# Tile 3's attention result turned by a DMA instead of TensorE, its low part one slot behind the join

## The chip, the core and the metric

The kernel runs on one core of a Trainium2 chip. The metric is the device time of one execution in microseconds (us), median over runs. TensorE (PE in the profile, its weight loads PEld) multiplies matrices, VectorE (DVE), ScalarE (ACT) and GpSimd (POOL) work on elements, SyncE (SP) issues nearly all DMAs. Each engine runs its own instructions in program order and waits on semaphores for the others.

## What is computed

A transformer block on 2048 positions of 512 numbers: attention with 32 heads of 16 numbers over 8 positions, two apart, then an MLP with a squared relu of 1792 hidden numbers. The reference, cut:

```python
def _A_ref(x, wqkv, wo):                    # H = 32, Dh = 16, W = 8, dil = 2
    q, k, v = split(x @ wqkv)
    idx = pos[:, None] - (arange(W) * dil)[None, :]      # 8 earlier positions
    logits = einsum("bhsd,bhswd->bhsw", q, k[idx]) * Dh ** -0.5
    attn = softmax(where(idx >= 0, logits, -1e9))
    o = einsum("bhsw,bhswd->bhsd", attn, v[idx])
    return o.reshape(B, S, D) @ wo
def _B_ref(x, w1, b1, w2, b2):
    r = relu(x @ w1 + b1)
    return (r * r) @ w2 + b2
h = x + _A_ref(layernorm(x), wqkv, wo)
out = h + _B_ref(layernorm(h), w1, b1, w2, b2)
```

## The kernel before

The 2048 positions are 16 tiles of 128. Every float32 product is made of three: each operand is split into a high part in a form that TensorE takes at full rate (a cast, `hi`, L151, on ScalarE) and a low part, the rest (a subtraction, `lo`, L154, on VectorE or GpSimd), and `mm3` (L221) multiplies high by high, low by high and high by low, 12 matmuls of 512 columns for a tile.

The work has two stages. In the first, TensorE makes q, k and v of all tiles, four tiles ahead and then two at a time (`first_phase`, L1040, for tiles 4 and 5 up to 14 and 15). In the second, the MLP runs over four sub-blocks of four tiles. Attention itself is elementwise work: VectorE multiplies and reduces (`dots`, `weigh`), GpSimd adds up (`add_up`), and it runs through the first stage and most of the second as a stream of steps beside the matmuls. Windows of k and v are read back from HBM for it by SP.

A tile's way from attention to the MLP: its result o is transposed, split into oh and ol, multiplied by wo (`wo_product`, L703), added to the residual (h), normalized (hn), transposed again and split into the parts hh and hl that the MLP's first product moves (in the tiles named big_l there). The product's order is set by `lows_last`: for tile 3, whose number is not in `OV`, first oh by wo's high part, then ol by wo's high part, then oh by wo's low part.

There are two ways to transpose o:

- By TensorE (`o_T`, L605): four transposes of 128x128 through the identity into PSUM, then the cast and the subtraction read PSUM.
- By DMA: `o_split` (L642) lets ScalarE write the 16-bit halves of the float32 numbers into two planes (tile pl), `turn_dma` (L631) transposes the planes back into o by a transposing DMA from SP, `o_join` (L647) lets ScalarE put the halves together again in pl, after which the cast and the subtraction read SBUF.

Before, tiles 0 to 3 go by TensorE and tiles 4 to 15 by DMA.

The order of the instructions is set by slots, stretches of TensorE work. In the first stage a slot is half of a 12-matmul product. What is to be done beside is put in lists: `at` runs at the slot's end, before the attention steps, `midway` (list `amid`) amid these steps, and `after` behind them. `end_slot` (L122) then lets `pump` (L420) append attention steps until VectorE's planned time catches up with TensorE's planned time:

```python
    def end_slot(pe):
        now["pe"] += pe
        run(due)
        pump()
        run(amid)
        run(late)
        now["slot"] += 1
```

`transposes` (L201) books 0.44 us of planned TensorE time, so the number of transposes also decides how many attention steps a slot takes. In `first_phase`, k counts the slots from the start of tiles 12 and 13: `OT` gives the slots in which tiles 0 to 3 are turned (4, 5, 10, 12) and `WO` those of their wo products (7, 9, 13, 15).

Of the kernel before, what the change touches and what calls it, by code (L numbers as in the profile page):

```python
# [19 lines left out]
R = 4  # L20
# [20 lines left out]
WO = 7, 9, 13, 15  # L41
HT = 20, 20, 21, 23
HK = (12, 18), (14, 19)
W2 = (18,)
LH = 3, 4, 10, 11
OP = 6, 7, 12, 13
# [12 lines left out]
def block_kernel(ctx, tc, x, wqkv, wo, w1, b1, w2, b2, out):  # L59
# [42 lines left out]
    def row(name, shape=(P, D), dt=F32):  # L102
        return work.tile(list(shape), dt, name=name, tag="row", bufs=ROWS)
# [9 lines left out]
    def at(delta, fn, *a):  # L113
        due.setdefault(now["slot"] + delta, []).append((fn, a))

    def after(delta, fn, *a):
        late.setdefault(now["slot"] + delta, []).append((fn, a))
# [4 lines left out]
# [7 lines that stand above are left out]
# [7 lines left out]
    def dve(t):  # L136
        now["dve"] += t
# [63 lines left out]
    def transposes(src, banks="tr"):  # L201
        tr = turn[banks].tile("tr").rearrange("p (k c) -> p k c", k=KB)
        for k in range(KB):
            nc.tensor.transpose(tr[:, k, :], src[:, k * P:(k + 1) * P], ident)  # L204
        now["pe"] += 0.44
        return tr
# [5 lines left out]
    def hi_T(tr, h_dst):  # L212
        for d, src in parts(tr, h_dst):
            hi(d, src)
# [205 lines left out]
    def pump(until=None):  # L420

        while (done[until] < G) if until is not None else (now["dve"] < now["pe"]):
            if until is None and now["dve"] > now["pe"] - HALF:
                run(amid)
            todo = sums[:]
            sums.clear()
            t = next(stream, "end")
            for a in todo:
                add_up(*a)
            if t == "end":  # L430
                now["dve"] = 1e9
                return
            if t is None:
                now["dve"] = max(now["dve"], now["pe"])
                return
            dve(t * SLOW[min(now['sub'] + 1, 2)])
# [40 lines left out]
    def x_T(t):  # L477
        tr = transposes(xt.pop(t))
        xT[t] = row("xh", (P, KB, P), F32R), row("xl", (P, KB, P), F32R)
        at(0, hi_T, tr, [xT[t][0]])  # L480
        (midway if t >= 6 else after)(0, lo_T, tr, [xT[t][0]], [xT[t][1]])
# [61 lines left out]
    def qkv_of(t, c, mid):  # L543

        ps = turn["mm"].tile("mm")
        xh, xl = xT[t]
        cs = slice(c * D, (c + 1) * D)
        mm3(ps, lambda k: xh[:, k, :], lambda k: xl[:, k, :],
            lambda k: wq_h[:, k, cs], lambda k: wq_l[:, k, cs], mid, 3 * KB // 2,
            lows_last=True)  # L550
        at(1, evac, t, 0, c, ps)
# [43 lines left out]
    oT = {}  # L595
# [9 lines left out]
    def o_T(t):  # L605
        s, j = divmod(t, RI)
        pump(until=s)
        tr = transposes(o_t[s][:, j, :])
        if t % R == RI:

            ohl = att.tile([P, 2, KB, P], F32R, name="ohl", tag="o", bufs=3)
            oT[t] = ohl[:, 0], ohl[:, 1]
        else:
            oT[t] = row("oh", (P, KB, P), F32R), row("ol", (P, KB, P), F32R)
        at(0, hi_T, tr, [oT[t][0]])
        at(0, lo_T, tr, [oT[t][0]], [oT[t][1]])
# [19 lines left out]
    def turn_join(key):  # L636
        src, pl = planes[key]
        nc.scalar.copy(halves_of(pl).rearrange("p two n -> p n two"),
                       two_planes(src).rearrange("p two n -> p n two"))
        planes[key] = pl.rearrange("p (k c) -> p k c", k=KB)  # L640
# [6 lines left out]
    def o_join(t, n=0):  # L647
        turn_join(("o", t))
        tr = planes.pop(("o", t))
        if t % R == RI:  # L650
            ohl = att.tile([P, 2, KB, P], F32R, name="ohl", tag="o", bufs=3)
            oT[t] = ohl[:, 0], ohl[:, 1]
        else:
            oT[t] = row("oh", (P, KB, P), F32R), row("ol", (P, KB, P), F32R)
        hi_T(tr, [oT[t][0]])
        (at if n or t >= 12 else midway)(n, lo_T, tr, [oT[t][0]], [oT[t][1]])

    def h_split(t):
        turn_split(("h", t), hn.pop(t))
# [43 lines left out]
    def wo_product(t, slots):  # L703
        ps = turn["mm"].tile("wo")
        oh, ol = oT.pop(t)
        mm3(ps, lambda k: oh[:, k, :], lambda k: ol[:, k, :],
            lambda k: wo_h[:, k, :], lambda k: wo_l[:, k, :], lows_last=t in OV)
        for n, (fn, a) in zip(slots, ((h_add, (t, ps)), (h_norm, (t,)), (add_b2, (t,)),
                                      (spill, (t,)))):
            (at if fn is h_add or fn is h_norm and t >= 14  # L710
             else midway if fn is h_norm and t in (6, 10) else after)(n + (fn is add_b2), fn, *a)
# [6 lines left out]
    def h_T(t):  # L718
        if t // R == R - 1:
            return last_h_T(t)  # L720
        tr = transposes(hn.pop(t), "mm")
        i = t % R
        hs_, ls_ = [a[:, :, i] for a in hh], [a[:, :, i] for a in hl]
        if len(turn["mm"].tags) > 2:
            at(0, hi_T, tr, hs_)
        else:
            due.setdefault(now["slot"], []).insert(0, (hi_T, (tr, hs_)))
        at(0, lo_T, tr, hs_, ls_)
# [281 lines left out]
    for n in range(16):  # L1010
        gp, t = divmod(n, 4)
# [28 lines left out]
    def first_phase(t0):  # L1040
        def chores(m):
            if t0 + 3 < 16:
                if m in (0, 2):
                    at(0, x_stats, t0 + 2 + m // 2)

                early = t0 == 12
                if m + early in ((4, 6) if t0 == R else (6, 7)):
                    at(0, x_norm, t0 + 2 + (m + early) // 7 if t0 > R else t0 + m // 2)
                if m in XT[early]:
                    x_T(t0 + 2 + XT[early].index(m))  # L1050
            if t0 + 5 < 16 and m in (6, 9):
                at(0, load_x, t0 + 2 + m // 3)
            if jobs and m % 3 == 0:
                at(0, weight_job)
            k = t0 // 2 * 12 - 72 + m
            if k == 19:
                dve(HOLD)
            for t in range(R):
                if k == OT[t]:
                    at(0, load_h, t)  # L1060
                    o_T(t)
                if t in HV and k == HK[t][0]:
                    at(0, h_split, t)
                    after(0, turn_dma, ("h", t))
                if t in HV and k == HK[t][1]:
                    at(0, turn_join, ("h", t))
                if k == WO[t]:
                    wo_product(t, (1, 3, 4, 6))
                    now["pe"] += 2.73
                if k == HT[t]:  # L1070
                    (at(0, h_parts, t) if t in HV else h_T(t))
            if k in W2:
                at(0, load_w2, W2.index(k))

        def half(m):
            end_slot(1.37)
            chores(m)

        for n in range(6):
            chores(2 * n)  # L1080
            qkv_of(t0 + n % 2, n // 2, lambda: half(2 * n + 1))
            end_slot(1.37)
# [40 lines left out]
    for u in range(R - 1):  # L1123
# [11 lines left out]
        for i in js:  # L1135
            t = R * (u + 1) + i
# [158 lines left out]
```

## Time and profile before

| | us |
|---|---|
| median of 3 runs | 501.18 |
| lowest and highest of them | 501.14, 502.29 |
| the profiled execution | 500.91 |
| its span, first to last instruction | 499.1 |
| TensorE busy in the span | 494.2 |
| VectorE busy | 383.7 |
| GpSimd busy | 354.6 |
| ScalarE busy | 305.7 |

The granted TensorE clock was 1.00 of full speed over the whole span. Busy time is summed over the span; which engine sets the time in a stretch is read from the chain and from the waits. All times below are from the span's start.

### The profile page before, as it was taken

Reading aid. Unit: us, or ns where it says so; the run is one execution under the profiler, and the core shown is the slowest. Engines: PE = TensorE matmul, PEld = TensorE weight load, DVE = VectorE, ACT = ScalarE, POOL = GpSimd, SP = SyncE. Lnnn points to the kernel's source line nnn. Section 1 sums busy time; section 2 is a strip of 40 time slices with the busy share of each in tenths; the row PEclk is TensorE's granted clock in tenths of the full one; section 3 lists DMA queues with packets and bytes.
Section 4 is the critical chain, followed back from the end, with each engine's and each line's share of the span. In section 5 each row is a group of like instructions: output and inputs, shape, how many; then the busy total and the mean of one; then the engine's idle time right before and its main releaser. Section 6 shows DMA issues by size and latency. Waiting matters only on the chain.

```text
span 499.1 us, 7514 instructions
## 1 busy us (share of the span) xinstructions
PE 494.2 (99%) x2411; PEld 420.6 (84%) x2411; DVE 383.7 (77%) x526; ACT 305.7 (61%) x543; POOL 354.6 (71%) x429
## 2 busy tenths in 40 slices
PE   8999999999999999999999999999999999999997
PEld 7998888888888888888888888888888888998986
DVE  6479899999989989998979989897984257733233
ACT  4634778668346757478564556866454968766551
POOL 5714798996775999888878777787889353885610
PEclk9999999999999999999999999999999999999999
DMA  8779979889788899689776945977680575355212
GB/s 269 201 215 244 281 253 297 272 268 310 209 219 260 294 286 259 185 226 248 219 253 210 218 143 164 269 236 258 201 202 14 130 193 163 117 158 169 64 42 87
DMA packets 113584, 103.67 MB, mean 208 GB/s; under 512 B 33672, under 2 KB 82056, under 8 KB 113544
## 3 DMA queue, kind: packets, MB, share of 16 engines
q1 hardware_dynamic: 112600, 102.66, 70.1%
q10 hardware_dynamic: 944, 0.52, 0.3%
q8 instruction: 19, 0.31, 0.3%
q14 instruction: 21, 0.17, 0.1%
HBM read 72.65 MB, written 24.25 MB: 194 GB/s over the span
## 4 chain that ended last, share of the span: by engine, by line
PE 98%; DMA 1%; ACT 0%; ACTq 0%; DVE 0%; issue 0%
PE mm L231 49%; PE acc L924 30%; PE wo L231 9%; PE mm L837 7%; PE tr L204 2%; DMA wraw<-in_A_wqkv_dram 1%; PE half L947 0%; ACTq L570 0%; ACT big_h L152 0%; ACT xh L152 0%; DVE h L949 0%
## 5 line engine op out<-in xcount | busy, mean ns | idle before, releaser
L414 POOL TENSOR_TENSOR pr<-pr 128x512 f32<-128x512 f32 (+1 forms) x128 | 134.1, 1048 | 35.6 <-DVE pr L357 30.2
L231 PE MATMUL mm<-big_l,w_h 128*128 128x512 f32 x336 | 88.5, 390 | 0.0
L357 DVE TENSOR_TENSOR pr<-ex,v 128x1024 f32<-128x1024 f32 x62 | 75.6, 1221 | 12.0 <-POOL o L414 9.2
L344 DVE TENSOR_TENSOR pr<-qp,k 128x1024 f32<-128x1024 f32 x64 | 76.8, 1200 | 6.1 <-ACT qp L271 3.3
L380 DVE TENSOR_REDUCE ex<-pr 128x64 f32<-128x1024 f32 x64 | 78.4, 1225 | 1.8
L231 PEld LDWEIGHTS mm<-big_l,w_h 128*128 128x128 f32 x336 | 63.0, 188 | 13.4 <-ACT r L894 0.3
L155 POOL TENSOR_TENSOR rl<-r,rh 128x512 fp32r<-128x512 f32 x42 | 54.9, 1306 | 24.2 <-ACT rh L152 20.1
L231 PE MATMUL mm<-big_l,xh 128*128 128x512 f32 (+1 forms) x208 | 56.3, 379 | 0.0
L231 PE MATMUL mm<-big_h,xh 128*128 128x512 f32 (+1 forms) x208 | 53.1, 377 | 0.3 <-ACT xh L152 0.3
L231 PE MATMUL mm<-big_h,xl 128*128 128x512 f32 (+1 forms) x208 | 52.6, 374 | 0.0
L924 PE MATMUL acc<-big_h,rh 128*128 128x512 f32 x190 | 52.1, 391 | 0.0
L924 PE MATMUL acc<-big_l,rh 128*128 128x512 f32 x190 | 52.0, 390 | 0.0
L924 PE MATMUL acc<-big_h,rl 128*128 128x512 f32 x190 | 51.7, 390 | 0.0
L231 PE MATMUL mm<-big_l,w_l 128*128 128x512 f32 x168 | 44.9, 389 | 0.0
L231 PEld LDWEIGHTS mm<-big_h,xl 128*128 128x128 f32 x208 | 38.3, 188 | 6.0
L231 PEld LDWEIGHTS mm<-big_h,xh 128*128 128x128 f32 x208 | 37.9, 188 | 6.1 <-ACT xh L152 0.5
L924 PEld LDWEIGHTS acc<-big_h,rl 128*128 128x128 f32 x190 | 35.7, 188 | 7.4
L924 PEld LDWEIGHTS acc<-big_l,rh 128*128 128x128 f32 x190 | 35.6, 188 | 7.4
L231 PEld LDWEIGHTS mm<-big_l,xh 128*128 128x128 f32 x208 | 37.4, 188 | 4.9
L924 PEld LDWEIGHTS acc<-big_h,rh 128*128 128x128 f32 x190 | 35.1, 188 | 7.1 <-DVE h L932 0.3
L894 ACT ACTIVATE r<-mm,b_sb 128x512 f32<-128x512 f32 x42 | 28.7, 684 | 16.2 <-PE mm L231 15.7
L231 PEld LDWEIGHTS mm<-big_l,w_l 128*128 128x128 f32 x168 | 31.5, 188 | 6.6
(167 smaller groups left out, 919.4 us busy)
## 6 DMA issues: line engine op xcount, KB each, us to landing
k<-qkv_d SPq DMA_DIRECT2D x50, 288.0 KB, 3.2
v<-qkv_d SPq DMA_DIRECT2D x46, 288.0 KB, 3.2
qkv_d<-y SPq DMA_DIRECT2D x18, 512.0 KB, 4.0
big_l<-w2l_d SPq DMA_DIRECT2D x24, 256.0 KB, 3.1
xt<-in_A_x_dram SPq DMA_DIRECT2D x16, 256.0 KB, 4.2
q<-qkv_d SPq DMA_DIRECT2D x32, 128.0 KB, 3.6
h<-in_A_x_dram SPq DMA_DIRECT2D x16, 256.0 KB, 3.3
h_d<-h SPq DMA_DIRECT2D x16, 256.0 KB, 3.4
```

The source lines that it names most:

```text
L155: eng.tensor_tensor(out=dst, in0=src, in1=h, op=ALU.subtract)
L204: nc.tensor.transpose(tr[:, k, :], src[:, k * P:(k + 1) * P], ident)
L231: nc.tensor.matmul(ps, l(k), r(k), start=(n == 0), stop=(n == 3 * KB - 1))
L344: nc.vector.tensor_tensor(out=pr.rearrange("p i w h d -> p i w (h d)"), in0=qps["now"][:, j % 2].unsqueeze(2).to_broadcast([P, RI, W, GC]) ...
L357: nc.vector.tensor_tensor(out=p2, in1=vwin, op=ALU.mult, in0=e1[:, :, :, j * GH:(j + 1) * GH].unsqueeze(4).to_broadcast([P, RI, W, GH, DH]))
L380: nc.vector.tensor_reduce(out=lf[:, :, :, j * GH:(j + 1) * GH], in_=pr, axis=X, op=ALU.add)
L414: nc.gpsimd.tensor_tensor(out=dst, in0=p2[:, :, :w], in1=p2[:, :, w:2 * w], op=ALU.add)
L837: nc.tensor.matmul(ps, sta[y][:, k], mov[x][:, k], start=(first and q == 0), stop=(last and q == len(terms) - 1), skip_group_check=True)
L894: nc.scalar.activation(r, ps, AF.Relu, bias=b1_sb[:, f:f + 1])
L924: nc.tensor.matmul(acc[j], l[:, j * P:(j + 1) * P], w[f], start=(first and n < len(js)), stop=(last and n >= len(terms) - len(js)))
```

## The change

Tile 3 leaves `o_T` and takes the way of tiles 4 to 15: its split and its DMA are issued behind the attention steps of slot 9, its join behind those of slot 12 (its transposes stood at the start of slot 12). With n = 1 and t below R, `o_join` puts the low part into the list `amid` of the next slot. The load of h for tile 3 stays where it was.

```diff
+OK = {3: (9, 12)}
...
         hi_T(tr, [oT[t][0]])
-        (at if n or t >= 12 else midway)(n, lo_T, tr, [oT[t][0]], [oT[t][1]])
+        (midway if t < R else at if n or t >= 12 else midway)(n, lo_T, tr, [oT[t][0]], [oT[t][1]])
...
             for t in range(R):
                 if k == OT[t]:
                     at(0, load_h, t)
-                    o_T(t)
+                    if t not in OK:
+                        o_T(t)
+                if t in OK and k == OK[t][0]:
+                    after(0, o_split, t)
+                    after(0, turn_dma, ("o", t))
+                if t in OK and k == OK[t][1]:
+                    after(0, o_join, t, 1)
```

The rows below show what stands on an engine in order, before and after; after, the line numbers of the helpers are one higher.

ScalarE from slot 9 to the evacuation of slot 13, before. y is the evacuation of a q, k or v product, hn a normalization, pl<-hn the split of another tile's h:

```order
L271 COPY qp<-q 128x256
L536 COPY y_90<-mm 128x8x64
L152 CAST ohl<-tr 128x512
L199 ACTIVATE hn<-h,rs 128x512
L152 CAST w_h<-raw 128x448
L536 COPY y_90<-mm 128x8x64
L629 COPY pl<-hn 128x1024
L152 CAST oh<-tr 128x512
L199 ACTIVATE hn<-h,rs 128x512
L271 COPY qp<-q 128x256
L536 COPY y_90<-mm 128x8x64
L629 COPY pl<-hn 128x1024
```

And now, in the same place:

```order
L272 COPY qp<-q 128x256
L630 COPY pl<-o 128x1024
L537 COPY y_90<-mm 128x8x64
L153 CAST ohl<-tr 128x512
L200 ACTIVATE hn<-h,rs 128x512
L153 CAST w_h<-raw 128x448
L537 COPY y_90<-mm 128x8x64
L630 COPY pl<-hn 128x1024
L200 ACTIVATE hn<-h,rs 128x512
L639 COPY pl<-o 128x1024
L153 CAST oh<-pl 128x512
L272 COPY qp<-q 128x256
```

The split of tile 3 (pl<-o) now stands ahead of an evacuation, and the join and the cast from pl stand behind the second normalization, where the cast from PSUM (oh<-tr) stood ahead of it.

VectorE at the same time, before. pr and ex are attention's products and logits, ol the low part, h the add of the residual:

```order
L155 TENSOR_TENSOR ohl<-tr,ohl 128x512
L344 TENSOR_TENSOR pr<-qp,k 128x1024
L155 TENSOR_TENSOR ol<-tr,oh 128x512
L357 TENSOR_TENSOR pr<-ex,v 128x1024
L380 TENSOR_REDUCE ex<-pr 128x16x4
L389 TENSOR_TENSOR ex<-ex,mask 128x256
L357 TENSOR_TENSOR pr<-ex,v 128x1024
L397 TENSOR_REDUCE mx<-ex 128x32
L399 TENSOR_TENSOR ex<-ex,mx 128x256
L674 TENSOR_TENSOR h<-wo,h 128x512
L163 BN_STATS st<-h 128x6
L164 BN_AGGR mv<-st 128x2
```

And now:

```order
L156 TENSOR_TENSOR ohl<-tr,ohl 128x512
L345 TENSOR_TENSOR pr<-qp,k 128x1024
L358 TENSOR_TENSOR pr<-ex,v 128x1024
L381 TENSOR_REDUCE ex<-pr 128x16x4
L156 TENSOR_TENSOR ol<-pl,oh 128x512
L390 TENSOR_TENSOR ex<-ex,mask 128x256
L358 TENSOR_TENSOR pr<-ex,v 128x1024
L675 TENSOR_TENSOR h<-wo,h 128x512
L164 BN_STATS st<-h 128x6
L165 BN_AGGR mv<-st 128x2
L398 TENSOR_REDUCE mx<-ex 128x32
L400 TENSOR_TENSOR ex<-ex,mx 128x256
```

The low part reads pl and stands behind an attention product and a reduction that stood behind it; the add of h and its statistics stand ahead of two softmax steps that were ahead of them.

VectorE at the end of the first stage, where the low parts of h for the MLP's first sub-block (big_l) are made, tiles 0 and 1 from pl, tiles 2 and 3 from PSUM (tr), before:

```order
L357 TENSOR_TENSOR pr<-ex,v 128x1024
L380 TENSOR_REDUCE ex<-pr 128x16x4
L155 TENSOR_TENSOR big_l<-pl,big_l 128x2x128 x4
L155 TENSOR_TENSOR big_l<-tr,big_l 128x2x128 x2
L344 TENSOR_TENSOR pr<-qp,k 128x1024
L155 TENSOR_TENSOR big_l<-tr,big_l 128x2x128 x2
L357 TENSOR_TENSOR pr<-ex,v 128x1024
L380 TENSOR_REDUCE ex<-pr 128x16x4
```

And now:

```order
L358 TENSOR_TENSOR pr<-ex,v 128x1024
L156 TENSOR_TENSOR big_l<-pl,big_l 128x2x128 x4
L156 TENSOR_TENSOR big_l<-tr,big_l 128x2x128 x2
L381 TENSOR_REDUCE ex<-pr 128x16x4
L345 TENSOR_TENSOR pr<-qp,k 128x1024
L156 TENSOR_TENSOR big_l<-tr,big_l 128x2x128 x2
L358 TENSOR_TENSOR pr<-ex,v 128x1024
L381 TENSOR_REDUCE ex<-pr 128x16x4
```

One reduction that stood ahead of all low parts now stands between those of tile 2 and those of tile 3. Further on, single attention steps and chores change places in the same way on VectorE, GpSimd, ScalarE and SP up to the third sub-block of the MLP; on TensorE the four transposes are gone and nothing else differs. On SP the new DMA stands between a load of a v window and the load of h for tile 2.

## Rows read from the trace of the kernel before

**Rows 1.** The page's chain that ended last, by engine.

```profile
PE 98%; DMA 1%; ACT 0%; ACTq 0%; DVE 0%; issue 0%
```

**Rows 2.** Waits of PE after its start: who for whom, us, times, longest.

```profile
PE mm L231 <- ACT xh L152: 0.3, 1, 0.3
```

**Rows 3.** One stage by windows: busy us (instructions) per engine, clock, DMA.

```profile
159.00:247.00 88.00, 88.00 (x392) 72.85 (x391) 81.32 (x98) 60.41 (x99) 78.11 (x84) 1.00 0.83 240
```

**Rows 4.** Timeline, PE around tile 3's transposes: start, us, instruction, count.

```profile
135.48 1.08 PE L231 MATMUL mm<-big_h,xl 128*128 128x512 f32 x4
...
136.40 0.60 PE L204 MATMUL tr<-ident,o 128*128 128x128 f32 x4
...
138.23 1.98 PE L231 MATMUL wo<-wo_h,ohl 128*128 128x512 f32 x8
```

**Rows 5.** Groups of instructions, shapes apart: busy us, mean ns, idle before.

```profile
L638 ACT COPY pl<-o 128x1024 uint16<-128x1024 uint16 x12 | 14.0, 1171 | 3.0 <-DMA o<-pl 3.0
...
L152 ACT CAST oh<-pl 128x512 fp32r<-128x512 f32 x9 | 5.6, 621 | 0.3
...
L380 DVE TENSOR_REDUCE ex<-pr 128x64 f32<-128x1024 f32 x64 | 78.4, 1225 | 1.8
```

**Rows 6.** Tile ol, VectorE's two forms: ns min/median/max.

```profile
L155 DVE TENSOR_TENSOR ol<-pl,oh x9: 681/967/1749, 199.0 to 395.7; 128x512 fp32r<-128x512 f32 x9
...
L155 DVE TENSOR_TENSOR ol<-tr,oh x3: 680/691/691, 119.2 to 138.7; 128x512 fp32r<-128x512 f32 x3
```

**Rows 7.** Line 633, the transposing DMAs: ns to issue, us to landing.

```profile
L633 SPq DMA_TRANSPOSE o<-pl x12: 1237/1237/3657, 191.2 to 388.6; - x12
...
DMA to landing us min/median/max: 2.7/3.9/4.9
```

**Rows 8.** Timeline around tile 3's turn and its wo product; idle before in brackets.

```profile
132.32 0.32 SPq L250 DMA_DIRECT2D v<-qkv_d  x1
...
133.39 0.59 ACT L536 COPY y<-mm 128x512 f32<-128x512 f32 x1 [4.10 <-PE mm L231]
...
136.83 0.32 SPq L250 DMA_DIRECT2D k<-qkv_d  x1
...
138.50 0.83 ACT L199 ACTIVATE hn<-h,rs 128x512 f32<-128x512 f32 x1
...
138.65 0.69 DVE L155 TENSOR_TENSOR ol<-tr,oh 128x512 fp32r<-128x512 f32 x1 [1.85 <-ACT oh L152]
...
142.51 0.59 ACT L536 COPY y<-mm 128x512 f32<-128x512 f32 x1 [2.90 <-PE mm L231]
...
143.67 1.07 PE L231 MATMUL wo<-wo_h,oh 128*128 128x512 f32 x4
...
144.58 1.07 PE L231 MATMUL wo<-wo_h,ol 128*128 128x512 f32 x4
```

**Rows 9.** Timeline at the start of the MLP.

```profile
154.93 2.97 DVE L155 TENSOR_TENSOR big_l<-pl,big_l 128x256 fp32r<-128x256 f32 x4 [0.61 <-ACT big_l L152]
...
159.61 0.74 DVE L155 TENSOR_TENSOR big_l<-tr,big_l 128x256 fp32r<-128x256 f32 x2
...
161.41 1.98 PE L231 MATMUL mm<-big_l,w_h 128*128 128x512 f32 x8
```

**Rows 10.** Timeline of the last part of attention and what follows it.

```profile
339.68 1.30 POOL L155 TENSOR_TENSOR rl<-r,rh 128x512 fp32r<-128x512 f32 x1 [4.07 <-ACT rh L152]
...
347.49 1.23 DVE L357 TENSOR_TENSOR pr<-ex,v 128x1024 f32<-128x1024 f32 x1 [2.54 <-POOL o L414]
...
384.70 1.05 ACT L629 COPY pl<-o 128x1024 uint16<-128x1024 uint16 x1 [7.07 <-POOL o L414]
...
385.65 0.68 ACT L894 ACTIVATE r<-mm,b_sb 128x512 f32<-128x512 f32 x1
...
386.39 1.20 PE L231 MATMUL mm<-big_l,w_h 128*128 128x512 f32 x4
...
387.42 1.08 PE L231 MATMUL mm<-big_l,w_l 128*128 128x512 f32 x4
```

## The prediction

> **What bounds the kernel.** I read the chain that ended last first, then TensorE's own waits, then busy time by stage, and only then single instructions. The chain is 98% TensorE [rows 1]: the kernel lasts as long as its matmuls do, plus the start and the end. Outside the start TensorE waited on a semaphore once that the profile sees, for 0.3 us [rows 2]. In the stage from 159 to 247 us it is busy 88.00 of 88 us, and VectorE, the next, 81.32 [rows 3]. So there are two ways in which an edit can move the time: it takes work off TensorE, which counts in full, or it makes an operand or a bank of TensorE late, which counts from the moment at which it is later than its use. Idle time of the other engines is no stock to gain from. The profiled execution took 500.91 us for a span of 499.1 us; the sum below is made against 500.91, and the median of the runs, 501.18, lies 0.27 us above it.
>
> **What is removed.** Four TensorE transposes of tile 3. Their price is read around them [rows 4]. Undisturbed, four matmuls of 512 columns take 0.91 us (143.67 to 144.58 in [rows 8]), 0.227 us each. The group ahead of the transposes starts at 135.48, and the wo product of tile 2 starts ten matmuls later, at 138.23. Ten matmuls are 2.27 us, so without the transposes it would have started at 137.75. The four cost 0.48 us. No wait of TensorE stands in this stretch. Term: minus 0.48 us.
>
> The Trainium skill, VectorE: DVE Perf Modes, section "The three transpose paths", gives TensorE 390 ns for a 128x128 block of bf16; four of these would be an estimated 1.56 us and the sum 499.35 us. The rows show less than a third of that, and the rows decide.
>
> **What is added for tile 3.** ScalarE gets two 16-bit copies, about 1.05 us (a split, as at 384.70 in [rows 10]) and 1.171 us (the join), and its cast now reads SBUF and takes 0.621 us [rows 5]. SyncE gets one transposing DMA: 1.24 us to issue, at most 3.66, and 2.7 to 4.9 us to land [rows 7]. VectorE's low part now has both inputs in SBUF: 0.68 to 1.75 us, where it was 0.68 to 0.69 with one in PSUM [rows 6]. None of this is TensorE's, so each counts nothing as long as its cover holds:
>
> - The split lies in slot 9, ahead of the evacuation at 133.39, before which ScalarE stood idle 4.10 us [rows 8]. 1.05 fits. Its source is long complete: the transposes of tile 2, which need the same steps of attention, waited for nothing. Without that cover the evacuations behind it would come 1.05 us later.
> - The DMA stands on SP behind the v load issued at 132.32, and ahead of a load of h and of the k load issued at 136.83 [rows 8]. 4.2 us lie free there, which 1.24 to 3.66 us fit into. Issued at about 132.7, it lands by 137.6 even with the longest landing.
> - Join and cast stand behind the second normalization, which ended at 138.50 + 0.83 = 139.33 [rows 8] and now ends some 0.6 us sooner, at 138.7, since the old cast stood ahead of it. So the high part is there at 138.7 + 1.17 + 0.62 = 140.5. Queued behind are the copy of q and the evacuation of 142.51, before which ScalarE was idle 2.90 us [rows 8]; 1.79 us fit.
> - VectorE no longer waits 1.85 us for the old cast at 138.65 [rows 8]. It runs an attention product and a reduction first, and takes the low part behind them. I bound its start by their old end, about 141.7 (138.65 + 0.69 and two steps of 1.2), so it ends at 142.4 to 143.5.
> - TensorE wants the high part at 143.67 and the low part at 144.58 [rows 8], both 0.48 sooner now: 143.19 and 144.10. Slack: 2.7 us for the high part and 0.6 to 1.7 us for the low one. Term: 0.
>
> **What moves.** The planner had booked 0.44 us of TensorE time for the transposes, and without it some attention steps start a slot later from there on. The order shows single steps that change places with the chore beside them (adds of h, low parts, weight splits), the chore now ahead. That is the safe direction for TensorE: what it waits for comes sooner, attention later. At two places that could still cost.
>
> First, the start of the MLP. There a reduction of 1.225 us [rows 5] now stands between tile 2's and tile 3's low parts of h. By the old times [rows 9] VectorE begins the first low parts at 154.93, where it waited 0.61 us for ScalarE. Tile 3's would start at 159.61 + 1.23 = 160.84, and its halves (0.41 us each) would be ready at 161.25 and 161.58. TensorE first uses them at 161.41 and, two matmuls later, at 161.86. Slack 0.16 and 0.28 us where it was 1.4. All of it hangs on TensorE's own progress, so it holds in the new times too. Cost 0; at worst, if one part ahead is held by as much more as the slowest low part of rows 6 is over the quickest (1.07 us), 1.07 - 0.16 = 0.9 us. The four parts at 154.93 already took 2.97 us, so much of such holding is in the old times, and I take 0.
>
> Second, the end of attention. ScalarE stood 7.07 us before the split of tile 14, waiting for GpSimd's last sum; behind it came an evacuation of 0.68 us, and with its end the matmuls at 386.39 began, which took 1.03 us to the next group instead of 0.91 [rows 10]. So TensorE loses 0.12 us here already, and whatever the end of attention slips is lost one for one. But the chain that leads there hangs on TensorE: GpSimd's low part at 339.68 waited 4.07 us for ScalarE, which had followed a matmul, and at 347.49 VectorE waited 2.54 us for GpSimd [rows 10]. A step of 1.2 us that comes later is absorbed in these waits, and the chain starts 0.48 us sooner with TensorE and ends so. Term: 0; the bounds are 0 and the 0.48 us that are lost if its end stays where it was.
>
> **Sum.** 500.91 - 0.48 = 500.43 us for a profiled execution, and 501.18 - 0.48 = 500.70 us for the median.
>
> **Rivals.**
>
> - The gain is given back: no change. If the end of attention stays at the same microsecond, the loss of 0.12 us at 386 becomes 0.60 and the time 501.18; the thin slack at the start of the MLP can take as much, at its worst 501.18 - 0.48 + 0.9 = 501.6. For it: both places are within half a microsecond of the edge. Against it: the waits of 4.07 and 2.54 us, behind which the chain starts anew. 501.0 to 501.6 us.
> - Slower: the end of attention slips by more than its slack. It decides from 2.54 us on, where VectorE in place of GpSimd sets the chain behind 347.49. Four steps late (4.9 us) would cost 2.4 us: 501.18 - 0.48 + 2.4 = 503.1 us. For it: nothing absorbs a slip behind the split of tile 14. Against it: the order shows one step at a place, not four.
> - The long path is late for tile 3's product. From split to low part it takes 1.05 + 4.9 + 1.17 + 0.62 + 1.75 = 9.5 us at its longest. If VectorE came to the low part 2.5 us later than I have it, the product would wait 0.8 to 1.9 us: 501.5 to 502.6 us. Against it: the waits of ScalarE and VectorE in rows 8, into which it falls. The Trainium skill, VectorE: DVE Perf Modes, section "Rules for kernel authors", speaks for this rival: TensorE for a 128x128 transpose where a result in PSUM will do, the DMA otherwise; no run here shows yet what the rule would cost.
> - The change doesn't do what it says: the transposes were hidden anyway, and the time stays at 501.18. Rows 4 exclude that.
>
> **How the numbers follow.** Forecast 0.60 (500.70; its own range 500.5 to 500.9). Gain given back 0.27. Attention's end slips 0.06. Tile 3 late 0.05. Something not thought of 0.02. The range takes the first two cases whole and the lower part of the late tile: 500.3 to 501.8. 0.3% of this kernel, 1.5 us, is about what a measurement can tell from no change. The first two cases and half of the late tile lie within it: 0.89 for the same. Slower takes the slipping, the rest of the late tile and a part of the unknown: 0.09. Faster by 1.5 us has no mechanism, since TensorE has no waits to give: 0.02.
>
> **What would show it.** Right: the ten matmuls from the group at 135.5 to tile 2's product in 2.27 us; no wait of TensorE for tile 3's high or low part; tile 3's low parts of h written before their matmuls; the matmuls behind the split of tile 14 about 0.5 us sooner, with the same 0.12 us. Wrong: a wait of TensorE on VectorE at the start of the MLP, the group at 386 taking over 1.3 us, or ScalarE standing for the new DMA past 141.

## The result, and the profile after

The changed kernel takes 502.44 us (median of 11 executions, 502.03 to 503.78) against 501.18 for the kernel before beside it (median of 11, one of them 2848.61): ratio 1.0027, 95% interval 1.0015 to 1.0039. The forecast was 500.70. So it is 1.26 us slower where 0.48 us were to be gained. That lies within the 0.3% taken for "the same", and outside the range of 500.3 to 501.8. The profiled execution took 502.22 us for a span of 500.4 us. Seven of the 11 executions lie between 502.03 and 502.50 and four between 503.38 and 503.78; the profiled one is of the first group, and no trace shows what the others lost.

The four transposes brought what they should. The timeline of the changed kernel at the place of [rows 4, 8], with start, length, engine, line, instruction and the idle time before it in brackets (... stands for lines left out):

```profile
135.47 1.08 PE L232 MATMUL mm<-big_h,xl 128*128 128x512 f32 x4
...
137.75 1.98 PE L232 MATMUL wo<-wo_h,ohl 128*128 128x512 f32 x8
...
138.74 1.16 ACT L639 COPY pl<-o 128x1024 uint16<-128x1024 uint16 x1
...
139.93 0.62 ACT L153 CAST oh<-pl 128x512 fp32r<-128x512 f32 x1
...
140.64 0.76 DVE L156 TENSOR_TENSOR ol<-pl,oh 128x512 fp32r<-128x512 f32 x1 [1.45 <-ACT oh L153]
...
143.19 1.07 PE L232 MATMUL wo<-wo_h,oh 128*128 128x512 f32 x4
...
144.09 1.07 PE L232 MATMUL wo<-wo_h,ol 128*128 128x512 f32 x4
```

From the group at 135.47 to tile 2's product are 2.28 us, where it was 2.75. Tile 3's high part ends at 140.55 and its low part at 141.40, for matmuls that start at 143.19 and 144.09. The whole new path is hidden.

What is new stands in TensorE's waits (who for whom, us, times, longest):

```profile
PE tr L205 <- ACT hn L200: 0.4, 1, 0.4
PE mm L232 <- ACT r L895: 0.2, 1, 0.2
```

Neither was there before [rows 2]. Busy time by window tells where: in the stage of [rows 3], where TensorE had been busy 88.00 of 88 us, it is now

```profile
159.00:247.00 88.00, 87.37 (x387) 71.79 (x386) 76.69 (x96) 60.26 (x98) 77.06 (x83) 1.00 0.82 235
```

The chain that ended last now leaves TensorE twice. The first time it is away from 150.2 to 167.6 us; the last pieces of that detour (start, length, engine, what):

```profile
157.94 1.15 DVE ex L381
159.12 1.08 DVE pr L345
160.20 0.66 DVE big_l L156 x2
160.86 1.14 DVE pr L358
162.00 0.02 issue
162.02 0.32 SPq L251
162.34 0.05 issue
162.39 3.96 DMA raw<-in_B_w_dram
166.35 0.02 issue
166.37 0.62 ACT big_h L153
167.00 0.59 ACT r L895
167.59 0.04 issue
167.63 3.01 PE mm L232 x12
```

Read from its end: the fourth group of 12 matmuls of the MLP's first product waits for the PSUM bank of the second, which ScalarE empties from 167.00 on (L895). That evacuation stands behind a cast of w2 (166.37), the cast behind a load of w2 (162.39), the load on SP's queue behind a load of v for attention (162.02), and that behind an attention product of VectorE (160.86), which came later because a reduction (157.94) now lies between the low parts of tile 2 and those of tile 3 (160.20), where it had been run before those of tiles 0 to 2. More is lost than the 0.2 us of wait, since the weight loads of these matmuls wait for the same evacuation (0.9 us in two).

The second time is at the start of the second pass:

```profile
227.77 2.73 PE wo L232 x12
...
230.53 0.70 DVE h L675
...
232.16 1.12 DVE pr L358
...
245.01 0.82 ACT hn L200
...
245.88 0.66 PE tr L205 x4
...
249.76 2.35 PE mm L232 x9
```

VectorE's add of tile 6's wo product (230.53) waited for TensorE, and an attention product (232.16) is now queued behind it. With that product GpSimd's sums come later, behind them the statistics of tile 7, its normalization on ScalarE, and TensorE's transposes of it. Then the low parts are late as well: the group at 249.76 starts 1.09 us behind the one before it (248.67), not 0.91.

Both detours show the same on VectorE. A chore now stands ahead of an attention step, but what the chore waits for comes no sooner, so VectorE stands idle in front of it and runs the step afterwards. The two places, and a third one at 219.96, in the changed kernel:

```profile
154.44 2.83 DVE L156 TENSOR_TENSOR big_l<-pl,big_l 128x256 fp32r<-128x256 f32 x4 [1.91 <-ACT big_l L153]
...
219.96 0.69 DVE L156 TENSOR_TENSOR big_l<-raw,big_h 128x512 fp32r<-128x512 f32 x1 [2.02 <-ACT big_h L153]
...
230.53 0.69 DVE L675 TENSOR_TENSOR h<-wo,h 128x512 f32<-128x512 f32 x1 [1.19 <-PE wo L232]
```

In the kernel before, the first idle time was 0.61 us [rows 9], and at the other two one reads

```profile
219.53 0.68 DVE L155 TENSOR_TENSOR big_l<-raw,big_h 128x512 fp32r<-128x512 f32 x1
...
230.55 0.69 DVE L674 TENSOR_TENSOR h<-wo,h 128x512 f32<-128x512 f32 x1 [0.40 <-PE wo L231]
```

The step that used to fill this time was the reduction at the first place and an attention product at the other two.

To add this up I take the starts of four of TensorE's groups in the profiled execution of each kernel, less the difference with which TensorE passes 111 us in it (up to 0.39 us). The kernel before has them at 138.39, 170.64, 334.84 and 484.94 us. Plus is later than before:

| kernel | at 138 | at 170 | at 335 | at 485 | median, beside before |
|---|---|---|---|---|---|
| changed | -0.47 | +0.02 | +0.94 | +1.03 | 502.44, 501.18 |
| changed, booked (e1) | -0.45 | -0.45 | -0.34 | -0.30 | 500.75, 501.14 |
| before, not booked (e2) | 0.00 | +0.39 | +1.30 | +1.42 | 502.45, 501.14 |
| booked late (e3) | -0.47 | 0.00 | -0.05 | +0.01 | 501.34, 501.14 |
| booked, taken off late (e4) | -0.48 | -0.48 | +0.42 | +0.55 | 502.04, 501.14 |
| first swap undone (e5) | -0.47 | -0.48 | +0.43 | +0.53 | 501.94, 501.09 |

The first row is the whole case: 0.48 gained, 0.49 lost at 167, 0.92 from 245 to 252, and 0.09 at 339, where the third pass of the MLP has begun and a group starts 1.89 us behind the one before it (337.44) and not 1.81. The last 0.2 to 0.3 us lie behind TensorE's last matmul, in the landing of the last output (3.0 us from VectorE's last add to the end of the span, 2.7 in the kernel before).

### The profile page after: what moved, and what is told of

It is laid out like the page before. It is cut to its first block, busy times and chain, and to the rows that moved or that the text cites. A ratio compares the mean times of both kernels' runs of the same rounds, so it can differ in the third digit from the quotient of the medians.

```text
span 500.4 us, 7509 instructions
## 1 busy us (share of the span) xinstructions
PE 494.8 (99%) x2407; PEld 420.4 (84%) x2407; DVE 381.7 (76%) x526; ACT 308.3 (62%) x545; POOL 354.6 (71%) x429
## 4 chain that ended last, share of the span: by engine, by line
PE 92%; POOL 2%; DVE 2%; ACT 1%; DMA 1%; issue 1%; SPq 0%; POOLq 0%; DVEq 0%
PE mm L232 46%; PE acc L925 28%; PE wo L232 8%; PE mm L838 7%; PE tr L205 2%; POOL pr L415 1%; PE tr L979 1%; DMA raw<-in_B_w_dram 1%; DVE big_l L156 1%; POOL rl L156 1%; DVE pr L358 0%; ACT pl L639 0%; ACT hn L200 0%; PE half L948 0%; POOL rs L172 0%
## 5 line engine op out<-in xcount | busy, mean ns | idle before, releaser
L895 ACT ACTIVATE r<-mm,b_sb 128x512 f32<-128x512 f32 x42 | 28.7, 684 | 18.1 <-PE mm L232 17.7
```

Of the source, the lines that this page charges most:

```text
L895: nc.scalar.activation(r, ps, AF.Relu, bias=b1_sb[:, f:f + 1])
```

## The experiments

The theory, T1: the loss comes from the order of the steps. With four transposes less, the planner has 0.44 us less of TensorE time on its books, so it starts attention steps later among the chores. The rival, R1: it comes from tile 3's own path, two more copies on ScalarE, a DMA, and a low part with both inputs in SBUF.

### The order and the path, taken apart

**e1.** The changed kernel with the time of the transposes still booked. Every queue then has the order of the kernel before, but for tile 3's own steps.

```diff
                     if t not in OK:
                         o_T(t)
+                    else:
+                        now["pe"] += 0.44
```

> The changed kernel, with the 0.44 us of TensorE time still booked at slot 10 where tile 3's transposes stood. Every engine then has the order of the kernel before, but for tile 3's own turn by DMA. Theory T1 (the swapped order costs, tile 3's own path costs nothing): the four transposes are saved and nothing else moves, 501.18 - 0.48 = 500.7 us, and no wait of TensorE at 167 and at 245. Rival R1 (tile 3's own path costs: two more copies on ScalarE, a DMA on SP, a low part with both inputs in SBUF): as the changed kernel, 502.4 us.

Measured: 500.75 us, ratio 0.9994 (0.9985 to 1.0003). TensorE's waits at 167 and 245 are gone; in the stage it is busy as before:

```profile
159.00:247.00 88.00, 88.00 (x392) 72.86 (x391) 78.08 (x99) 60.52 (x98) 79.19 (x84) 1.00 0.82 242
```

**e2.** The kernel before, its transposes kept, their time taken off the books.

```diff
                     o_T(t)
+                    if t == 3:
+                        now["pe"] -= 0.44
```

> The kernel before, with tile 3's four transposes still on TensorE, but not booked (0.44 us taken off at slot 10). The order of every engine is that of the changed kernel, but for tile 3's own turn. T1: the loss at 167 us falls away, since TensorE comes there 0.48 us later than in the changed kernel, where it waited 0.36 to 0.49; the loss at 245 (0.92) and that of the tail (0.1 to 0.4) stay: 502.1 to 502.5 us. R1: as the kernel before, 501.2 us.

Measured: 502.45 us, ratio 1.0033 (1.0020 to 1.0045): as slow as the changed kernel with not one instruction removed. The two runs together decide against R1. That the time fell into the expected range was luck, since the sum was wrong inside: the loss at 167 did not fall away, 0.39 us of it stayed (the table). Both detours begin at TensorE and end at it, so they shift with it, and a TensorE that comes later doesn't find them done.

**e3, e4.** The 0.44 us booked only from the fifth slot of the MLP's first pass on (e3), or up to it (e4), in the loop over p with u = 0:

```diff
+            if (u, p) == (0, 4):
+                now["pe"] += 0.44      # e3, on the changed kernel
+                now["pe"] -= 0.44      # e4 in its place, on e1
```

> The changed kernel, with the 0.44 us booked at the fifth slot of the MLP's first pass. The order up to there is that of the changed kernel (the reduction between tile 2's and tile 3's low parts of h among it), behind it that of the kernel before. T1, with two separate losses: the wait at 167 stays and eats the 0.48 us of the transposes, the wait at 245 is gone: 501.1 to 501.3 us. If the second loss followed from the first, and not from the order behind it: 502.4. R1: 502.4 us.

> The changed kernel, with the 0.44 us booked at slot 10 and taken off again at the fifth slot of the MLP's first pass. The order is that of the kernel before up to there, and that of the changed kernel behind it. T1: no wait at 167, the wait at 245 stays: 500.7 + 0.92 = 501.6 us, up to 502.1 if GpSimd's statistics of tile 7 do not come sooner with TensorE. If the second loss followed from the first: 500.7. R1: 502.4 us.

Measured: e3 501.34 us (ratio 0.9996 to 1.0014), e4 502.04 (1.0016 to 1.0034). The table has each loss alone: e3 keeps the first (0.47) and none of the second, e4 the second (0.90) and none of the first. They are two, and each follows from the order in its own stretch.

### Single swaps

**e5, e6, e7.** The changed kernel, with 0.44 us booked for one slot and taken off in the next: slot 19 (e5), slot 12 of the MLP's first pass (e6), or both (e7).

```diff
+            if k in (19, 20):
+                now["pe"] += 0.44 if k == 19 else -0.44     # e5, e7
...
+            if u == 0 and p in (12, 13):
+                now["pe"] += 0.44 if p == 12 else -0.44     # e6, e7
```

> The changed kernel with 0.44 us booked for one slot only, slot 19 of the numbered ones, and taken off in the next. That restores one pair of steps: VectorE's reduction of an attention product stands again ahead of the six low parts of h's tiles 0 to 2, and on GpSimd a sum ahead of an add. All else is as in the changed kernel. T1 (this swap alone is behind the wait at 167 us): the first loss, 0.49 us, is gone and the second stays: 501.95 us. If that wait came from the other swaps ahead of it or from tile 3's own path: 502.4 us.

> The changed kernel with 0.44 us booked in slot 12 of the MLP's first pass and taken off in the next. On VectorE that restores one pair: the attention product of the weights and v stands again ahead of the add that takes in tile 6's wo product; on SyncE a few loads go with it. T1 (this swap alone is behind the wait at 245): the second loss goes, 502.44 - 0.91 = 501.5 us, and the wait at 167 stays. If the wait at 245 came from the other swaps of this pass: 502.4 us.

> Both single swaps undone, all other swaps of the changed kernel left in. T1: both losses gone, 502.44 - 0.49 - 0.91 = 501.0 us, and 500.75 (as with the whole booking) if the tail of 0.1 to 0.3 us goes too. If the many other swaps matter: 501.5 to 502.4 us.

Measured: e5 501.94 us (1.0017 to 1.0035). That it met the expected 501.95 to a hundredth is luck at this spread, but the table shows the first loss gone whole: one reduction of 1.23 us in front of the low parts or behind them, with the sum on GpSimd that moves with it, makes it. e6 501.84 (1.0009 to 1.0026): the second swap gives 0.4 to 0.5 us back, not 0.91, so neither expectation held. e7 501.41 (1.0000 to 1.0020) lies between its two expectations as well.

So the second loss has another part. Some of it lies at the same place: in e6 TensorE still loses 0.52 of the 0.92 us there, with a wait of 0.24 us for tile 7's normalized h at 245.87. The swap at 219.96 is still in e6 and e7: VectorE stands idle for 2.01 us there in both, and not in e1. GpSimd's sums behind it, which began at 219.69 in the kernel before and at 219.29 in e1, begin at 222.56 and 221.69. It wasn't undone alone. Another part shows in e7's trace at the next start of a pass. Its profiled execution was one of its longer ones (502.43 us), and in it VectorE and GpSimd did this:

```profile
330.44 4.17 POOL L695 TENSOR_TENSOR h<-h,b_sb 128x512 f32<-128x512 f32 x3
...
330.55 4.68 DVE L156 TENSOR_TENSOR big_l<-pl,big_l 128x256 fp32r<-128x256 f32 x4
...
337.62 2.11 PE L232 MATMUL mm<-big_l,w_h 128*128 128x512 f32 x8 [0.91 <-DVE big_l L156]
```

Four low parts of h took 4.68 us, beside GpSimd's three adds of the bias (4.17 us). In the kernel before the same four took 1.36 (from 330.21), nearly all of it ahead of the adds (from 331.25). TensorE waited 0.91 us for what followed. The same execution had lost 0.4 us ahead of that, at the wo product at 323.13, where weight loads waited 0.54 us for ScalarE's high part.

### Is VectorE held by GpSimd's adds?

T2: low parts whose two inputs both lie in SBUF wait while GpSimd's adds of b2 run. R2: they only come late by their queue.

**e9, e10, e11.** Adds of b2 left out: of tiles 5 to 7 in the changed kernel (e9), of 5 to 7 and 9 to 11 in e7 (e10) and in e1 (e11).

```diff
     def add_b2(t):
+        if t in (5, 6, 7):
+            return
```

> The changed kernel without GpSimd's three adds of the bias b2 to tiles 5, 6 and 7 of h, which run from 244.9 to 249.1 us (the output lacks that bias in these tiles). Nothing ahead of 244.9 changes. Theory T2 (behind the late statistics, the second half of the loss at 245 is VectorE being held in its low parts of h, 2.85 us for two where it was 1.85, because GpSimd's adds read SBUF at that time): the two low parts take under 1.4 us, TensorE's group at 249.76 starts without delay, and of the 0.92 us some 0.45 stay (the wait of TensorE for tile 7's normalized h): 502.44 - 0.45 = 502.0 us. Rival R2 (these low parts only come late, by the queue ahead of them): 502.3 to 502.4 us.

> The kernel with both single swaps undone, and without GpSimd's adds of b2 to tiles 5, 6, 7, 9, 10 and 11 (the output lacks the bias there), those that ran beside VectorE's low parts of h at the two starts of a pass, 245 and 331 us. T2 (what is left of the loss with both swaps undone, 501.41 against 500.75 us, is VectorE held beside these adds, four low parts in 4.68 us at 330.55): 500.6 to 500.8 us, and the four low parts in under 1.6 us. R2 (it is the other swaps of attention steps): 501.3 us or more.

> The changed kernel with the 0.44 us booked, and without the same six adds (the output lacks the bias there): what the adds cost where the order is that of the kernel before. T2: some 0.1 to 0.2 us, the slow step between 247 and 334 us, 500.55 to 500.75 us. R2: 500.75 us, nothing.

Measured, with an output that lacks the bias in these tiles: e9 502.01 us (1.0014 to 1.0036), e10 501.02 (0.9994 to 1.0011), e11 500.69 (0.9984 to 1.0002). First the two rows of the changed kernel, the adds and the two low parts of tile 6:

```profile
244.94 4.15 POOL L695 TENSOR_TENSOR h<-h,b_sb 128x512 f32<-128x512 f32 x3
...
246.52 2.85 DVE L156 TENSOR_TENSOR big_l<-hnp,big_l 128x256 fp32r<-128x256 f32 x2
```

and of e9, the low parts and TensorE's groups behind them:

```profile
246.58 0.75 DVE L156 TENSOR_TENSOR big_l<-hnp,big_l 128x256 fp32r<-128x256 f32 x2
...
248.73 1.07 PE L232 MATMUL mm<-big_l,w_l 128*128 128x512 f32 x4
...
249.64 1.98 PE L232 MATMUL mm<-big_l,w_h 128*128 128x512 f32 x8
```

The same two instructions, at the same time behind the same queue, take 0.75 us without the adds and 2.85 with them, and the third group follows after 0.91 us again. TensorE's wait of 0.43 us for tile 7's normalized h stays (at 245.94), as T2 has it. (That the median met the expected 502.0 is closer than the spread of e9, 501.55 to 503.48, allows.) By the starts of TensorE's groups about 0.60 of the 0.92 us are lost before the new pass begins, in both kernels, and the other 0.32 in the low parts, in the changed kernel alone.

The kernel before holds the control. It ran the same adds, and the pair of tile 6 took 1.85 us in it, so one of the two parts was held there too, without a wait of TensorE. At its next start of a pass, low parts that read SBUF twice (pl) and low parts that read PSUM once (tr) ran beside the same three adds:

```profile
331.25 4.37 POOL L694 TENSOR_TENSOR h<-h,b_sb 128x512 f32<-128x512 f32 x3
...
332.63 1.84 DVE L155 TENSOR_TENSOR big_l<-pl,big_l 128x256 fp32r<-128x256 f32 x2
...
334.39 0.74 DVE L155 TENSOR_TENSOR big_l<-tr,big_l 128x256 fp32r<-128x256 f32 x2
```

The pair that reads PSUM took its usual 0.74 us beside an add. So T2 stands for the low parts, and as far as these rows go it is their second SBUF input that matters. Where the order is that of the kernel before, the adds cost nothing that can be measured (e11). e10 lies between T2 and R2: of the 0.66 us by which the median of e7 exceeds that of e1, 0.33 are left between e10 and e11, so the adds are about half of it as far as medians so close can tell. For the other half e10's trace offers a wait of 0.24 us for tile 7 at 245.33, as in the changed kernel, behind the swap that e6 and e7 had kept as well; that this swap makes it wasn't tried.

The Trainium skill, SBUF — State Buffer, section "Who interferes with whom", has this as a rule: a VectorE instruction with two SBUF inputs contends with a GpSimd instruction that reads SBUF, because its second input comes through a read interface that both share. These rows agree.

### Versions meant to be better

**e8.** e1 with tile 2 turned by DMA as well: `OK = {2: (8, 10), 3: (9, 12)}`.

> The changed kernel with the 0.44 us booked, and tile 2's result turned by DMA as well, split at slot 8 and joined at slot 10, its 0.44 us booked too. T1 (removed transposes count in full as long as the order stays): 500.75 - 0.46 = 500.3 us. Rival R1 (the path costs once its cover is thin: tile 2's high part is due about 1 us behind its cast, and a weight load and a k load stand behind the new DMA on SP): 500.8 to 502 us.

**e12, e14, e13.** The adds of b2, and the stores behind them, three slots later: in e8 for tiles 5, 6, 7, 9, 10, 11 (e12) or for 5, 6, 7 alone (e14), and in the changed kernel for 5, 6, 7 (e13).

```diff
-             else midway if fn is h_norm and t in (6, 10) else after)(n + (fn is add_b2), fn, *a)
+             else midway if fn is h_norm and t in (6, 10) else after)(
+                n + (fn is add_b2) + 3 * (fn in (add_b2, spill) and t in (5, 6, 7)), fn, *a)
```

> A version meant to be better: tiles 2 and 3 turned by DMA with their 0.88 us booked, and the six adds of b2 (and the stores of h behind them) three slots later, among attention's sums, where VectorE has no low part of h. T2: 500.63 less the 0.1 to 0.2 us of the held low parts: 500.4 to 500.6 us. R2, or if the moved adds hold attention's sums and products instead: 500.6 to 501.2 us.

> The version with tiles 2 and 3 turned by DMA and 0.88 us booked, with only the adds of tiles 5, 6 and 7 moved by three slots, those of 9, 10 and 11 left where they were. If the slow version lost its 1.9 us at the end of attention by the adds of 9 to 11 alone: 500.63 less some 0.1 to 0.2 us, 500.4 to 500.6 us, without a wait of TensorE for ScalarE at 387. If the adds of 5 to 7 took part: 501 us or more.

> The changed kernel with nothing left out and nothing booked, but the adds of b2 to tiles 5, 6 and 7 (and the stores behind them) three slots later, so that they no longer run beside VectorE's low parts of h at 246 us. T2: as without these adds, 502.0 us, the two low parts in under 1.4 us; what the moved adds hold among attention's sums is absorbed by the waits ahead of attention's end. Rival: the 3.9 us of adds among the sums of the second pass reach its end: 502.4 us or more.

Measured: e8 500.63 us (0.9982 to 1.0000), between the two expectations of 500.3 and 500.8. TensorE is 0.92 us ahead at 138 and 0.64 at 170: the place of the first loss takes a part again, its cast of w2 now being

```profile
165.90 0.62 ACT L153 CAST big_h<-raw 128x512 fp32r<-128x512 f32 x1 [2.12 <-DMA raw<-in_B_w_dram]
```

where the load kept ScalarE waiting 1.10 us in e1. e12: 502.34 us (1.0017 to 1.0040), beyond both of its expectations (at most 501.2), and slower by its second half: at 335 TensorE is still 0.56 us ahead. Its six moved adds went in among attention's sums, and at the end of attention, at the place of [rows 10], one reads

```profile
386.10 1.04 ACT L630 COPY pl<-o 128x1024 uint16<-128x1024 uint16 x1 [7.28 <-POOL o L415]
...
387.78 1.20 PE L232 MATMUL mm<-big_l,w_h 128*128 128x512 f32 x4 [1.37 <-ACT r L896]
```

The last sum comes late, and TensorE waits 1.37 us. e14, without the moved adds of tiles 9 to 11, has no such wait: 500.53 us beside 500.93 (0.9983 to 1.0001), as expected. e13 missed: 503.19 us (1.0029 to 1.0054) where 502.0 was expected. The rival's number (502.4 or more) came, but not its mechanism, since nothing is lost at the end of attention. Its low parts at 246.63 take 0.74 us, as without the adds, but at the next start of a pass the adds of 9 to 11 meet VectorE instead, and four low parts take 4.66 us from 331.79 on:

```profile
338.84 2.12 PE L232 MATMUL mm<-big_l,w_h 128*128 128x512 f32 x8 [0.91 <-DVE big_l L156]
```

Another 0.5 us is lost ahead of that, at the wo product at 324.43, which waits for its high part as in e7. What was mended at one start of a pass was lost at the next. The fastest versions, e14, e8 and e1, have intervals that reach to or just past 1: a gain of 0.4 us is likely and not proved.

## Why the prediction was wrong

**What is removed: right.** 0.48 us, measured as 0.47.

**What is added for tile 3: right.** Its high part was foreseen for 140.5 and came at 140.55; the low part came 1 us before the bound of 142.4. e1 prices the whole path: 500.75 for a forecast of 500.70, and TensorE 0.45 us ahead at 138 and at 170. The rival of the late tile 3 is out. What was cited for it (the Trainium skill, VectorE: DVE Perf Modes, section "Rules for kernel authors"), to turn a 128x128 block on TensorE where a result in PSUM will do, doesn't agree with these rows: for this tile the DMA's path cost nothing and TensorE's 0.48 us.

**What moves: wrong, and here the prediction failed.** Its step was: "the chore now ahead. That is the safe direction for TensorE: what it waits for comes sooner, attention later." Its cost was put at 0, and was 1.50 us by TensorE's groups. Both halves of the step failed. What TensorE waits for came no sooner, since the chore put ahead had to wait for its operand: tile 6's add began at 230.53 where it had begun at 230.55. And an attention step is not only attention's. Chores of TensorE hang behind it, on other queues than the one where the two change places. A load of v that comes late holds the load of w2 behind it on SP, that a cast on ScalarE, and that the evacuation of a bank: 0.49 us (e5: this swap alone). A product that comes late makes GpSimd's sums late, and the statistics queued behind them: 0.60 us with the wait of 0.43, and 0.32 through the low parts (e4, e9). The single swap that I took for its cause gives back about half (0.40 by TensorE's groups, e6); the swap at 219.96 makes GpSimd's sums late too, and its share is open. I had followed the swaps on the engine where they stood and at two places; the cost came at two others.

**The start of the MLP: the place was right and safe.** Tile 3's low parts began at 160.12 and TensorE's group at 160.93 did not wait. The price of being held, 1.07 us for one low part [rows 6], was about right for one part (2.1 us for two). But I had let one part be held at one start of a pass. At the start of the next pass, which I hadn't looked at, both parts of tile 6 were (2.85 us against 0.75).

**The end of attention: right.** The loss there is what it was: the matmuls at 387.38 take 1.04 us to the next group where it was 1.03 [rows 10]. The rival of a slipping end was not the cause here, but e12 made it real, one for one.

**The rivals.** The gain was given back, the second likeliest case, but not at its places and more than whole: 1.50 us lost for 0.48 gained. No case had two losses at once, so the range ended at 501.8. That the kernel stayed within 0.3% of the time before is no merit of the reasoning.

## What to carry to other kernels

Where a list of booked times decides the order, taking out work is two edits: the work and its booking. Try them apart; here the booking was worth nearly three times the work (1.31 us in e2, against 0.48), and putting 0.44 back on the books turned 502.44 into 500.75. A chore put ahead of another step is only sooner if its operand is there; look for the idle time in front of it and for the step that had filled it. When a step comes later, follow every queue behind it, the DMA queue's loads and GpSimd's statistics too, up to TensorE's next bank and operand; and look at each start of a pass, not only at the nearest one.

## What the runs showed of the hardware

VectorE's low parts with two SBUF inputs were held while GpSimd's adds ran beside them: two of 128x256 took 2.85 us instead of 0.75 (changed kernel, e9), four took 4.68 instead of 1.36 (e7, kernel before). Low parts with one input in PSUM were not: 0.74 us for two beside an add (kernel before, 334.39). How many parts are hit depends on a microsecond of order: one of the pair at 245 in the kernel before (1.85 us for two), where it cost TensorE nothing, both in the changed kernel, and three of four at the start behind that in e7 and e13 (4.68 and 4.66 us for four). The prediction's 1.07 us was the price of one such part; several in a row had no place in it.
